# Reordering the edges of a four-layer linear-attention and gated-MLP kernel: first tiles, norms, o tiles, last product

## Chip, cores, metric

One core of a Trainium2 chip. The metric is the device time in microseconds (us) of one execution, lower is better. PE is the matmul engine, DVE the vector engine, ACT the activation engine, POOL the general one, SP the queue that issues the DMAs. SBUF is the on-chip memory, PSUM the one that takes PE's sums. The granted clock is the share of PE's full clock that the profile shows. Tiles, groups and units are counted from 0: k(2,0) is the first half of tile 2's k product.

## The reference, cut

Four layers over x of 2048 x 1024 in bf16: A, B, A, B, each on a layer norm of x and added to x.

```python
def _A_ref(x, wqkv, wo):                 # linear attention, 32 heads of 32
    q, k, v = ...x @ wqkv...
    pq, pk = phi(q), phi(k)              # t > 0: t + 1, else exp(t); + 1e-6
    kv = jnp.einsum("bhsd,bhse->bhde", pk, v)
    z = jnp.einsum("bhsd->bhd", pk)
    num = jnp.einsum("bhqd,bhde->bhqe", pq, kv)
    den = jnp.einsum("bhqd,bhd->bhq", pq, z)[..., None] + 1e-6
    return (num / den)... @ wo
def _B_ref(x, w_gate, w_up, w_down):     # F = 3584
    return ((x @ w_gate) * (x @ w_up)) @ w_down
x = x + _A_ref(_layernorm(x), A_wqkv, A_wo); x = x + _B_ref(_layernorm(x), ...)   # twice
```

## The kernel before

x stays in SBUF as 16 tiles of 128 rows (four groups of four). A matmul unit accumulates 8 (or 28) matmuls of 512 columns into one of four PSUM buffers ("mm"); a fifth PSUM tile ("kv", one buffer) takes the kv products and later the o tiles. The order of the program is set by hand: lists of units, woven together: `weave(main, fill, first, step)` puts one piece of `fill` after unit `first` of `main` and after every `step`-th one from there, and the rest of `fill` at the end. In the traces the instructions of an engine follow each other in the order in which the units are called, on DVE also where a later one is ready first: in that of before ACT's part of a phi is done at 837.79 us, and DVE's part of it starts at 845.03, behind the statistics and applies called ahead of it. So the call order is read here as the queue order of each engine.

```python
def ln_stats(t):    # DVE: bn_stats twice, bn_aggr; POOL: add eps, power -0.5
def ln_apply(t):    # DVE: xn = (X[t] - mean) * rstd
def tx_pe(t):       # PE: eight 128x128 transposes of xn into PSUM; ACT: copy to xT
def tx(t, slot):    # the same transpose as one DMA on SP
def phi(ps, dst):   # ACT: e = exp(ps); DVE: e = min(e, 1) + 1e-6; dst = max(ps + 1 + 1e-6, e)
def k_unit(t, n):   # 8 matmuls, phi
def v_unit(t, n):   # 8 matmuls, ACT copy
def kv_unit(t):     # 8 matmuls of 132 columns into kv; after the last tile DVE: KVz = kv * mask
def q_unit(g, c):   # 8 matmuls, phi into pqT[g % 3]
def o_unit(t):      # 8 matmuls of 132 columns with KVz into kv; DVE: den + 1e-6, reciprocal, divide
def d_unit(t, n, last): # 28 matmuls, DVE: X += ps, and in the last layer the store

# ---- start of layer 0 (cut) ----
for t in range(TPG):                  # TPG = 4
    ln_stats(t)
    if t > 0:
        ln_apply(t - 1)
ln_apply(3)
ones()
make_mask()
tx_pe(0)()
for t in range(TPG):
    k_unit(t, 0)()
    if t < 3:
        tx_pe(t + 1)()
ts = range(TPG)
main = [k_unit(t, 1) for t in ts] + [v_unit(t, 0) for t in ts]
# ... v_unit(t, 1) and kv_unit(t - 1) follow
fill = []
for t in range(TPG, 2 * TPG):
    fill += [stats_unit(t), apply_unit(t), tx_pe(t)]
do(weave(main, fill, 1, 1))

# ---- o phase (cut) ----
do([q2[0], kv_unit(NT - 1), q2[1], q2[2], o0[0], q2[3], q2[4], o0[1], t0[0], q2[5], o0[2], t0[1], q2[6],
    q2[7], o0[3], ...])

# ---- last group of the down-projection, layer 1 (cut) ----
main = d_unit(t, 0), d_unit(t, 1), stats_unit(t) for each of the four tiles
fill = norm_fill(1, 1, True) + norm_fill(2, 2, True)     # 24 pieces: statistics, applies, transposes
do(weave(main, fill, 0, 1))                              # one piece after each unit, the rest at the end
```

Of the kernel before, what the change touches and what calls it, by code (L numbers as in the profile page):

```python
# [9 lines left out]
ALU = mybir.AluOpType  # L10
# [15 lines left out]
def kernel(  # L26
# [11 lines left out]
    nc = tc.nc  # L38
# [56 lines left out]
    def load(dst, src):  # L95
        nc.sync.dma_start(out=dst, in_=src)  # L96
# [7 lines left out]
    def load_q():  # L104
        for n in range(2):
            load(wq[n], wqkv_v[:, :, n * NB:(n + 1) * NB])

    def load_o():
        for n in range(2):
            load(wo[n], wo_v[:, :, n * NB:(n + 1) * NB])  # L110
# [7 lines left out]
        for i in range(KF // 4):  # L118
            load(Dr[i][:].rearrange("p (f n) -> p f n", n=D), wd_v[:, 4 * i:4 * i + 4, :])

    load(X[:, 0, :], x_view[:, 0, :])
    load(X[:, 1, :], x_view[:, 1, :])
    for k in range(0, KD, 2):
        load(wk[0][:, k:k + 2, :], wqkv_v[:, k:k + 2, D:D + NB])
    load(X[:, 2, :], x_view[:, 2, :])
    load(X[:, 3, :], x_view[:, 3, :])
    load_k(1)
    load_v(0)
    load_v(1)
    for t in range(TPG, 2 * TPG):  # L130
        load(X[:, t, :], x_view[:, t, :])
    load_q()
    for t in range(2 * TPG, NT):
        load(X[:, t, :], x_view[:, t, :])
    load_o()


    ident = const.tile([P, P], BF16, tag="ident", name="ident")
# [22 lines left out]
    def ln_stats(t):  # L161
        st = small.tile([P, 2, 6], F32, tag="st", name="st")
        for c in range(2):
            nc.vector.bn_stats(out=st[:, c, :], in_=X[:, t, c * NB:(c + 1) * NB])  # L164
        mv = small.tile([P, 2], F32, tag="mv", bufs=2 * TPG, name="mv")
        nc.vector.bn_aggr(out=mv[:], in_=st[:])
        ve = small.tile([P, 1], F32, tag="ve", name="ve")
        nc.gpsimd.tensor_scalar(out=ve[:], in0=mv[:, 1:2], scalar1=1e-5, scalar2=None, op0=ALU.add)
        rstd = small.tile([P, 1], F32, tag="rstd", bufs=2 * TPG, name="rstd")
        nc.gpsimd.tensor_tensor(out=rstd[:], in0=ve[:], in1=mhalf[:], op=ALU.pow)  # L170
        stat[t] = (mv, rstd)
# [3 lines left out]
    def ln_apply(t):  # L175
        mv, rstd = stat.pop(t)
        xn = work.tile([P, D], BF16, tag="xn", name="xn")
        nc.vector.tensor_scalar(out=xn[:], in0=X[:, t, :], scalar1=mv[:, 0:1], scalar2=rstd[:],
                                op0=ALU.subtract, op1=ALU.mult)
        xns[t] = xn  # L180
# [13 lines left out]
    def tx_pe(t):  # L194

        def run():
            if t not in xns:
                ln_apply(t)
            src = xns.pop(t)
            pt = psum.tile([P, KD, P], BF16, tag="mm", bufs=MM, name="pt")  # L200
            for k in range(KD):
                nc.tensor.transpose(out=pt[:, k, :], in_=src[:, k * P:(k + 1) * P], identity=ident[:])  # L202
            nc.scalar.copy(out=xT[t // TPG][:, :, t % TPG * P:(t % TPG + 1) * P], in_=pt[:])  # L203
        return run

    def mm_tile():
        return psum.tile([P, NB], F32, tag="mm", bufs=MM, name="ps")
# [15 lines left out]
    def k_unit(t, n):  # L223
        def run():
            ps = mm_tile()
            xt, tl = xT[t // TPG], t % TPG
            for k in range(KD):
                nc.tensor.matmul(out=ps[:], lhsT=xt[:, k, tl * P:(tl + 1) * P], rhs=wk[n][:, k, :],  # L228
                                 start=(k == 0), stop=(k == KD - 1))
            phi(ps, pk[t % 4][:, n * NB:(n + 1) * NB])  # L230
        return run
# [61 lines left out]
    def add_x(t, n, ps):  # L293
        nc.vector.tensor_tensor(out=X[:, t, n * NB:(n + 1) * NB], in0=X[:, t, n * NB:(n + 1) * NB],  # L294
                                in1=ps[:], op=ALU.add)
# [25 lines left out]
        return run  # L321

    def d_unit(t, n, last):
        def run():
            ps = mm_tile()
            tl = t % TPG
            for f in range(KF):
                nc.tensor.matmul(out=ps[:], lhsT=hT[:, f, tl * P:(tl + 1) * P], rhs=wd[f][:, n * NB:(n + 1) * NB],  # L328
                                 start=(f == 0), stop=(f == KF - 1))
            add_x(t, n, ps)  # L330
            if last:
                nc.sync.dma_start(out=o_view[:, t, n * NB:(n + 1) * NB], in_=X[:, t, n * NB:(n + 1) * NB])
        return run

    def stats_unit(t):
# [22 lines left out]
    def ones():  # L358
        for i in range(4):
            nc.gpsimd.memset(vz[i][:, :, P:ZW], 1.0)  # L360
# [8 lines left out]

    def layer_A(li):  # L370
        if li == 0:
            for t in range(TPG):
                ln_stats(t)
                if t > 0:
                    ln_apply(t - 1)
            ln_apply(3)
            ones()
            make_mask()
            tx_pe(0)()
            for t in range(TPG):  # L380
                k_unit(t, 0)()
                if t < 3:
                    tx_pe(t + 1)()
            ts = range(TPG)
            main = [k_unit(t, 1) for t in ts] + [v_unit(t, 0) for t in ts]
            for t in ts:
                main.append(v_unit(t, 1))
                if t > 0:
                    main.append(kv_unit(t - 1))
            fill = []  # L390
            for t in range(TPG, 2 * TPG):
                fill += [stats_unit(t), apply_unit(t), tx_pe(t)]
            do(weave(main, fill, 1, 1))
        else:
            ones()
            do(weave(kv_group(0), norm_fill(3, 3, False), 1, 2))
        do(weave(kv_group(1), norm_fill(2, 2, True) if li == 0 else [], 1, 1))
        do(q_group(0))
        do(weave(kv_group(2), norm_fill(3, 3, True) if li == 0 else [], 1, 1))
        do(q_group(1))  # L400
        do(kv_group(3))
        load_gu(0)
        load_gu(1)

        def o(g):
            return [o_unit(t) for t in range(g * TPG, (g + 1) * TPG)]

        def to(g):
            return [to_unit(t) for t in range(g * TPG, (g + 1) * TPG)]

        def out_group(g):
            return [u for t in range(g * TPG, (g + 1) * TPG) for u in (out_unit(t, 0), out_unit(t, 1))]

        o0, t0, o1, t1, o2, t2, o3, t3 = o(0), to(0), o(1), to(1), o(2), to(2), o(3), to(3)
        q2, q3 = q_group(2), q_group(3)
        do([q2[0], kv_unit(NT - 1), q2[1], q2[2], o0[0], q2[3], q2[4], o0[1], t0[0], q2[5], o0[2], t0[1], q2[6],
            q2[7], o0[3], t0[2], q3[0], q3[1], q3[2], o1[0], t0[3], q3[3], q3[4], o1[1], t1[0], q3[5],
            q3[6], o1[2], t1[1], q3[7]])
        s = [stats_unit(t) for t in range(TPG)]
        a = [apply_unit(t) for t in range(TPG)]  # L420
        x = [tx(t, 0) for t in range(TPG)]
        u = out_group(0)
        do([u[0], o1[3], t1[2], u[1], u[2], o2[0], t1[3], u[3], u[4], o2[1], u[5], u[6], o2[2], u[7]])
        u = out_group(1)
        do([t2[0], t2[1], t2[2], u[0], o2[3], u[1], t2[3], s[0], u[2], o3[0], u[3], s[1], u[4], o3[1], u[5], s[2],
            u[6], o3[2], u[7], s[3]])
        load_gu(2)
        u = out_group(2)
        do([t3[0], t3[1], u[0], o3[3], t3[2], u[1], a[0], u[2], t3[3], x[0], u[3], a[1], u[4], x[1], u[5], a[2],
            u[6], x[2], u[7], a[3]])  # L430
        do([x[3]] + out_group(3))

    def layer_B(li):
        last = li == 3
        load_d()
        nxt = norm_fill(1, 1, True)
        for g in range(NG):
            main = []
            for fb in range(FB):
                i = g * FB + fb  # L440
                main += [gu_unit(i, fb * 4 + j) for j in range(4)]
                main.append(prefetch(i, last))
            do(weave(main, nxt, 2, 1))
            nxt = []
            main = []
            for tl in range(TPG):
                t = g * TPG + tl
                main += [d_unit(t, 0, last), d_unit(t, 1, last)]
                if g == NG - 1 and not last:
                    main.append(stats_unit(t))  # L450
            if g == 0:
                nxt = norm_fill(2, 0, True)
            elif g == 1:
                nxt = norm_fill(3, 1, True)
            elif g == 2 and not last:
                nxt = norm_fill(0, 0, True)
            fill = []
            if g == 3 and not last:
                fill = norm_fill(1, 1, True) + norm_fill(2, 2, True)
            do(weave(main, fill, 0, 1))  # L460
        if not last:
            load_q()
            load_o()
# [48 lines left out]
```

## Time and profile before

1659.57 us median of four runs (1659.42 to 1659.61). The page of the profiled execution, its first two lines and the chain of waits by engine (busy us, share of the span, instructions):

```profile
span 1657.6 us, 18876 instructions
PE 1643.1 (99%) x8016; PEld 761.1 (46%) x8016; DVE 537.5 (32%) x963; ACT 254.1 (15%) x426; POOL 53.7 (3%) x152
PE 97%; DVE 1%; ACT 0%; DMA 0%; SPq 0%; issue 0%; POOL 0%; POOLq 0%
```

PE is the limit and hardly ever rests. Matmuls overlap (one of 512 columns is recorded as 379 ns long), so the 1643 us alone do not prove it, but the starts do: 216 ns from one 512-column matmul to the next and 56 ns for 128 columns. All that an order of instructions can win is the time in which PE stands. PE's own waits before (who waited for whom: us in total, times, longest):

```profile
PE ps L228 <- ACT xT_70 L203: 4.5, 4, 1.1
PE kv L276 <- DVE H L281: 2.6, 2, 1.3
PE pt L202 <- DVE xn L178: 2.0, 3, 1.3
PE zps L156 <- DVE xT_73 L153: 1.2, 1, 1.2
PE kv L252 <- DVE H L220: 0.8, 2, 0.5
```

This is the whole prize, about 10 us (the 1.2 us of zps, the dummy matmuls before X 0 lands, are no part of it; from start to start of the matmuls each gap is some 0.15 us longer than the wait as the page counts it, at the o tile 1.45 against 1.29). L228 is a k unit waiting for the copied transpose, L202 a transpose waiting for xn, L276 an o tile, L252 a kv product. PE's timeline of the start (start us, us, then the instructions; in brackets the idle time before):

```profile
6.76 0.62 PE L202 MATMUL pt<-ident,xn 128*128 128x128 bf16 x8 [0.28 <-DVE xn L178]
8.48 1.90 PE L228 MATMUL ps<-W_74,xT_70 128*128 128x512 bf16 x8 [1.10 <-ACT xT_70 L203]
10.80 0.62 PE L202 MATMUL pt<-ident,xn 128*128 128x128 bf16 x8 [0.42 <-DVE xn L178]
12.52 1.90 PE L228 MATMUL ps<-W_74,xT_70 128*128 128x512 bf16 x8 [1.10 <-ACT xT_70 L203]
29.66 0.62 PE L202 MATMUL pt<-ident,xn 128*128 128x128 bf16 x8 [1.35 <-DVE xn L178]
```

Each k unit has only its own tile, so PE waits four times for transpose and copy; at 29.66 tile 4's transpose waits for xn, whose statistics stood behind phi on DVE. The o phase of the first A layer (timeline):

```profile
168.45 0.63 PE L276 MATMUL kv<-KVz,D_80 128*128 128x132 bf16 x8
172.37 0.63 PE L276 MATMUL kv<-KVz,D_80 128*128 128x132 bf16 x8
174.74 1.23 DVE L281 TENSOR_TENSOR H<-kv,den 128x1024 bf16<-128x1024 f32 x1
176.02 0.64 PE L276 MATMUL kv<-KVz,D_80 128*128 128x132 bf16 x8 [1.29 <-DVE H L281]
```

Two q units lie between the first two o tiles and one between the second and third; the third needs the kv buffer, which DVE frees at 175.97. The second A layer begins like this:

```profile
846.10 0.41 PE L252 MATMUL kv<-H 128*128 128x132 bf16 x4 [0.31 <-DVE H L220]
847.03 0.41 PE L252 MATMUL kv<-H 128*128 128x132 bf16 x4 [0.52 <-DVE H L220]
```

The first kv product waits twice for phi (L220), which stood on DVE behind statistics and applies (836.07 to 845.12 us). And the tail:

```profile
1654.27 0.69 DVE L294 TENSOR_TENSOR X<-X,ps 128x512 bf16<-128x512 bf16 x1 [5.36 <-PE ps L328]
1654.99 0.33 SPq L332 DMA_DIRECT2D out_dram<-X  x1
```

The last add takes 0.69 us, and its store lands 1.70 us after its issue, at 1656.69.

### The profile page before, as it was taken

The numbers are of one execution on the slowest core, as the hardware profiler recorded it, in microseconds if no ns is written. First come the engines' busy times: TensorE is split into PE (matmuls) and PEld (weight loads), VectorE is DVE, ScalarE is ACT, GpSimd is POOL, SyncE is SP. The second block draws the span as 40 slices with busy tenths as digits, with TensorE's granted clock in tenths as the row PEclk, the third lists the DMA queues.
The fourth block names the chain that finished last, engine by engine and source line by source line (L and its number), as shares of the span: only waits on it lengthen the run. The fifth ranks groups of instructions, "written<-read, shape, count | busy, mean of one in ns | idle before, by whom it ended". The sixth has DMA issues, their size and how long they took to land.

```text
span 1657.6 us, 18876 instructions
## 1 busy us (share of the span) xinstructions
PE 1643.1 (99%) x8016; PEld 761.1 (46%) x8016; DVE 537.5 (32%) x963; ACT 254.1 (15%) x426; POOL 53.7 (3%) x152
## 2 busy tenths in 40 slices
PE   8999999999999999999999999999999999999999
PEld 3544444444444444444444445444444444444444
DVE  5453873211311321131353348631122113111111
ACT  3333201100110110011023331011001101100110
POOL 2000000000000000000110000000000000000000
PEclk9999999999999999999999999999999999999999
DMA  9111459530641353063260033594225405421400
GB/s 304 27 26 55 105 121 288 168 102 4 178 152 48 111 169 102 3 179 102 66 159 1 0 109 66 134 307 152 86 69 173 156 23 156 154 85 64 153 4 23
DMA packets 240483, 181.57 MB, mean 110 GB/s; under 512 B 96016, under 2 KB 231184, under 8 KB 240400
## 3 DMA queue, kind: packets, MB, share of 16 engines
q1 hardware_dynamic: 240400, 180.38, 37.6%
q8 instruction: 62, 1.02, 0.3%
q14 instruction: 21, 0.17, 0.0%
HBM read 153.09 MB, written 4.19 MB: 95 GB/s over the span
## 4 chain that ended last, share of the span: by engine, by line
PE 97%; DVE 1%; ACT 0%; DMA 0%; SPq 0%; issue 0%; POOL 0%; POOLq 0%
PE ps L316 47%; PE ps L328 23%; PE ps L302 7%; PE ps L265 6%; PE ps L238 6%; PE ps L228 6%; PE kv L252 1%; PE kv L276 1%; DVE st L164 1%; DMA X<-in_A_x_dram 0%; ACT xT_70 L203 0%; ACT H L218 0%; SPq L96 0%; PE pt L202 0%; DVE H L281 0%
## 5 line engine op out<-in xcount | busy, mean ns | idle before, releaser
L320 DVE TENSOR_TENSOR H<-gs,ps 128x512 bf16<-128x512 f32 x224 | 154.0, 688 | 567.7 <-PE ps L316 563.1
L319 ACT COPY gs<-ps 128x512 f32<-128x512 f32 x224 | 131.0, 585 | 1048.1 <-PE ps L316 1048.1
L328 PEld LDWEIGHTS <-H 128*128 128x128 bf16 x1792 | 175.3, 98 | 211.5
L294 DVE TENSOR_TENSOR X<-X,ps 128x512 bf16<-128x512 bf16 x128 | 87.3, 683 | 359.1 <-PE ps L328 330.4
L218 ACT ACTIVATE H<-ps 128x512 bf16<-128x512 f32 x128 | 76.4, 597 | 208.3 <-PE ps L228 99.6
L316 PEld LDWEIGHTS <-W_75 128*128 128x128 bf16 x640 | 62.6, 98 | 75.5
L316 PEld LDWEIGHTS <-W_74 128*128 128x128 bf16 x640 | 62.6, 98 | 75.5
L219 DVE TENSOR_SCALAR H<-H 128x512 bf16<-128x512 bf16 x128 | 37.3, 291 | 168.4 <-ACT H L218 168.4
L316 PEld LDWEIGHTS <-xT_73 128*128 128x128 bf16 x576 | 56.4, 98 | 67.9
L316 PEld LDWEIGHTS <-xT_72 128*128 128x128 bf16 x576 | 56.4, 98 | 68.0
L316 PEld LDWEIGHTS <-W_77 128*128 128x128 bf16 x576 | 56.4, 98 | 67.9
L316 PEld LDWEIGHTS <-W_76 128*128 128x128 bf16 x576 | 56.3, 98 | 68.0
L164 DVE BATCH_NORM_STATS2 st<-X 128x6 f32<-128x512 bf16 x128 | 80.9, 674 | 4.3 <-DMA X<-in_A_x_dram 4.3
L316 PE MATMUL ps<-xT_71,W_77 128*128 128x512 bf16 x320 | 75.6, 379 | 0.0
L316 PE MATMUL ps<-xT_71,W_74 128*128 128x512 bf16 x320 | 75.6, 379 | 0.0
L316 PE MATMUL ps<-xT_70,xT_72 128*128 128x512 bf16 x320 | 75.6, 379 | 0.0
L316 PE MATMUL ps<-xT_70,xT_73 128*128 128x512 bf16 x320 | 75.6, 379 | 0.0
L316 PE MATMUL ps<-xT_70,W_75 128*128 128x512 bf16 x320 | 75.6, 379 | 0.0
L316 PE MATMUL ps<-xT_71,W_76 128*128 128x512 bf16 x320 | 75.6, 379 | 0.0
L316 PE MATMUL ps<-xT_71,W_75 128*128 128x512 bf16 x320 | 75.6, 379 | 0.0
L316 PE MATMUL ps<-xT_70,W_74 128*128 128x512 bf16 x320 | 75.6, 379 | 0.0
L302 PEld LDWEIGHTS <-H 128*128 128x128 bf16 x512 | 49.4, 98 | 56.2
(88 smaller groups left out, 1715.0 us busy)
## 6 DMA issues: line engine op xcount, KB each, us to landing
W_74<-in_B_w_gate_dram SPq DMA_DIRECT2D x20, 1024.0 KB, 5.3
W_75<-in_B_w_up_dram SPq DMA_DIRECT2D x20, 1024.0 KB, 7.2
W_76<-in_B_w_gate_dram SPq DMA_DIRECT2D x18, 1024.0 KB, 5.3
W_77<-in_B_w_up_dram SPq DMA_DIRECT2D x18, 1024.0 KB, 7.3
xT_72<-in_B_w_gate_dram SPq DMA_DIRECT2D x18, 1024.0 KB, 5.3
xT_73<-in_B_w_up_dram SPq DMA_DIRECT2D x18, 1024.0 KB, 7.4
X<-in_A_x_dram SPq DMA_DIRECT2D x16, 256.0 KB, 7.8
out_dram<-X SPq DMA_DIRECT2D x32, 128.0 KB, 1.7
```

The costliest lines, as they stand in the source:

```text
L164: nc.vector.bn_stats(out=st[:, c, :], in_=X[:, t, c * NB:(c + 1) * NB])
L218: nc.scalar.activation(out=e, in_=ps[:], func=ACT.Exp)
L219: nc.vector.tensor_scalar(out=e, in0=e, scalar1=1.0, scalar2=1e-6, op0=ALU.min, op1=ALU.add)
L228: nc.tensor.matmul(out=ps[:], lhsT=xt[:, k, tl * P:(tl + 1) * P], rhs=wk[n][:, k, :], start=(k == 0), stop=(k == KD - 1))
L238: nc.tensor.matmul(out=ps[:], lhsT=xt[:, k, tl * P:(tl + 1) * P], rhs=wv[n][:, k, :], start=(k == 0), stop=(k == KD - 1))
L265: nc.tensor.matmul(out=ps[:], lhsT=wq[n][:, k, cl * P:(cl + 1) * P], rhs=xT[g][:, k, :], start=(k == 0), stop=(k == KD - 1))
L294: nc.vector.tensor_tensor(out=X[:, t, n * NB:(n + 1) * NB], in0=X[:, t, n * NB:(n + 1) * NB], in1=ps[:], op=ALU.add)
L302: nc.tensor.matmul(out=ps[:], lhsT=oT[(t // TPG) % 2][:, c, tl * P:(tl + 1) * P], rhs=wo[n][:, c, :], start=(c == 0), stop=(c == KD - 1))
L316: nc.tensor.matmul(out=ps[:], lhsT=w[:, k, j * P:(j + 1) * P], rhs=xT[g % 2][:, k, :], start=(k == 0), stop=(k == KD - 1))
L319: nc.scalar.copy(out=gs[:], in_=gp[:])
L320: nc.vector.tensor_tensor(out=hT[:, f, :], in0=gs[:], in1=up[:], op=ALU.mult)
L328: nc.tensor.matmul(out=ps[:], lhsT=hT[:, f, tl * P:(tl + 1) * P], rhs=wd[f][:, n * NB:(n + 1) * NB], start=(f == 0), stop=(f == KF - 1))
```

## The change

The intent is to take PE's waits away at four places: (1) the start: other order of the first loads and tiles, group 1's transposes by DMA instead of PE, the loads of wq, X 8 to 15 and wo after them; (2) the norms of the next A layer spread over the last down-projection, four pieces after each unit, instead of one piece a unit and the rest after it, with the statistics of group 3 moved from there into the A layer; (3) an o tile at every second q unit; (4) the last product in three parts, so that the last add and store are small.

```diff
-    load(X[:, 0, :], x_view[:, 0, :])
-    load(X[:, 1, :], x_view[:, 1, :])
+    load_x(0)
     for k in range(0, KD, 2):
         load(wk[0][:, k:k + 2, :], wqkv_v[:, k:k + 2, D:D + NB])
+        if k == 0:
+            load_x(1)
...                        (load_q, X 8 to 15 and load_o move behind the start, below)
     def d_unit(t, n, last):
+        parts = [(0, 256), (256, 384), (384, 512)] if last and (t, n) == (NT - 1, 1) else [(0, NB)]
...                        (matmuls, add and store once for each part)
         if li == 0:
-            (as printed above)
+            ln_stats(0)
+            ln_stats(1)
+            ln_apply(0)
+            ln_apply(1)
+            tx_pe(0)()
+            tx_pe(1)()
+            ln_stats(2)
+            ln_apply(2)
+            k_unit(0, 0)()
+            ln_stats(3)
+            ln_apply(3)
+            k_unit(1, 0)()
+            tx_pe(2)()
+            k_unit(0, 1)()
+            tx_pe(3)()
             ones()
             make_mask()
+            main = [k_unit(2, 0), k_unit(1, 1), k_unit(3, 0), k_unit(2, 1), k_unit(3, 1)]
+            main += [v_unit(t, 0) for t in ts]
...
+            do(weave(main, norm_fill(1, 1, True), 3, 1))     # DMA transposes
+            load_q()
+            for t in range(2 * TPG, NT):
+                load_x(t)
+            load_o()
         else:
             ones()
-            do(weave(kv_group(0), norm_fill(3, 3, False), 1, 2))
+            do(weave(kv_group(0), norm_fill(3, 3, True), 1, 2))
...
-        do([q2[0], kv_unit(NT - 1), q2[1], q2[2], o0[0], q2[3], q2[4], o0[1], t0[0], q2[5], o0[2], t0[1], q2[6], ...
+        do([q2[0], kv_unit(NT - 1), q2[1], o0[0], q2[2], q2[3], o0[1], t0[0], q2[4], q2[5], o0[2], t0[1], q2[6], ...
...                        (statistics of the last group leave the down-projection of layer B)
-            do(weave(main, fill, 0, 1))
+            for i, u in enumerate(main):
+                u()
+                do(fill[4 * i:4 * i + 4])
```

More of the change, by code (lines that the diff above doesn't have):

```diff
@@ L119, in load_d, with load_x @@
             load(Dr[i][:].rearrange("p (f n) -> p f n", n=D), wd_v[:, 4 * i:4 * i + 4, :])
-    load(X[:, 0, :], x_view[:, 0, :])
-    load(X[:, 1, :], x_view[:, 1, :])
+    def load_x(t):
+        load(X[:, t, :], x_view[:, t, :])
+    load_x(0)
     for k in range(0, KD, 2):
         load(wk[0][:, k:k + 2, :], wqkv_v[:, k:k + 2, D:D + NB])
-    load(X[:, 2, :], x_view[:, 2, :])
-    load(X[:, 3, :], x_view[:, 3, :])
+        if k == 0:
+            load_x(1)
+    load_x(2)
+    load_x(3)
     load_k(1)
@@ L130 @@
     for t in range(TPG, 2 * TPG):
-        load(X[:, t, :], x_view[:, t, :])
-    load_q()
-    for t in range(2 * TPG, NT):
-        load(X[:, t, :], x_view[:, t, :])
-    load_o()
+        load_x(t)
     ident = const.tile([P, P], BF16, tag="ident", name="ident")
@@ L323, in d_unit @@
     def d_unit(t, n, last):
+        parts = [(0, 256), (256, 384), (384, 512)] if last and (t, n) == (NT - 1, 1) else [(0, NB)]
         def run():
-            ps = mm_tile()
             tl = t % TPG
-            for f in range(KF):
-                nc.tensor.matmul(out=ps[:], lhsT=hT[:, f, tl * P:(tl + 1) * P], rhs=wd[f][:, n * NB:(n + 1) * NB],
-                                 start=(f == 0), stop=(f == KF - 1))
-            add_x(t, n, ps)
-            if last:
-                nc.sync.dma_start(out=o_view[:, t, n * NB:(n + 1) * NB], in_=X[:, t, n * NB:(n + 1) * NB])
+            for lo, hi in parts:
+                ps = mm_tile()
+                cols = slice(n * NB + lo, n * NB + hi)
+                for f in range(KF):
+                    nc.tensor.matmul(out=ps[:, 0:hi - lo], lhsT=hT[:, f, tl * P:(tl + 1) * P], rhs=wd[f][:, cols],
+                                     start=(f == 0), stop=(f == KF - 1))
+                nc.vector.tensor_tensor(out=X[:, t, cols], in0=X[:, t, cols], in1=ps[:, 0:hi - lo], op=ALU.add)
+                if last:
+                    nc.sync.dma_start(out=o_view[:, t, cols], in_=X[:, t, cols])
         return run
@@ L371, in layer_A @@
         if li == 0:
-            for t in range(TPG):
-                ln_stats(t)
-                if t > 0:
-                    ln_apply(t - 1)
+            ln_stats(0)
[8 more added lines that the diff above has]
+            ln_stats(3)
             ln_apply(3)
+            k_unit(1, 0)()
+            tx_pe(2)()
+            k_unit(0, 1)()
+            tx_pe(3)()
             ones()
             make_mask()
-            tx_pe(0)()
-            for t in range(TPG):
-                k_unit(t, 0)()
-                if t < 3:
-                    tx_pe(t + 1)()
             ts = range(TPG)
-            main = [k_unit(t, 1) for t in ts] + [v_unit(t, 0) for t in ts]
+            main = [k_unit(2, 0), k_unit(1, 1), k_unit(3, 0), k_unit(2, 1), k_unit(3, 1)]
+            main += [v_unit(t, 0) for t in ts]
             for t in ts:
@@ L389, in layer_A @@
                     main.append(kv_unit(t - 1))
-            fill = []
-            for t in range(TPG, 2 * TPG):
-                fill += [stats_unit(t), apply_unit(t), tx_pe(t)]
-            do(weave(main, fill, 1, 1))
+            do(weave(main, norm_fill(1, 1, True), 3, 1))
+            load_q()
+            for t in range(2 * TPG, NT):
+                load_x(t)
+            load_o()
         else:
             ones()
-            do(weave(kv_group(0), norm_fill(3, 3, False), 1, 2))
+            do(weave(kv_group(0), norm_fill(3, 3, True), 1, 2))
         do(weave(kv_group(1), norm_fill(2, 2, True) if li == 0 else [], 1, 1))
@@ L415, in layer_A @@
         q2, q3 = q_group(2), q_group(3)
-        do([q2[0], kv_unit(NT - 1), q2[1], q2[2], o0[0], q2[3], q2[4], o0[1], t0[0], q2[5], o0[2], t0[1], q2[6],
-            q2[7], o0[3], t0[2], q3[0], q3[1], q3[2], o1[0], t0[3], q3[3], q3[4], o1[1], t1[0], q3[5],
-            q3[6], o1[2], t1[1], q3[7]])
+        do([q2[0], kv_unit(NT - 1), q2[1], o0[0], q2[2], q2[3], o0[1], t0[0], q2[4], q2[5], o0[2], t0[1], q2[6],
+            q2[7], o0[3], t0[2], q3[0], q3[1], o1[0], t0[3], q3[2], q3[3], o1[1], t1[0], q3[4], q3[5], o1[2], t1[1],
+            q3[6], q3[7]])
         s = [stats_unit(t) for t in range(TPG)]
@@ L444, in layer_B @@
             nxt = []
-            main = []
-            for tl in range(TPG):
-                t = g * TPG + tl
-                main += [d_unit(t, 0, last), d_unit(t, 1, last)]
-                if g == NG - 1 and not last:
-                    main.append(stats_unit(t))
+            main = [d_unit(g * TPG + tl, n, last) for tl in range(TPG) for n in range(2)]
+            fill = []
             if g == 0:
@@ L456, in layer_B @@
                 nxt = norm_fill(0, 0, True)
-            fill = []
-            if g == 3 and not last:
+            elif g == 3 and not last:
                 fill = norm_fill(1, 1, True) + norm_fill(2, 2, True)
-            do(weave(main, fill, 0, 1))
+            for i, u in enumerate(main):
+                u()
+                do(fill[4 * i:4 * i + 4])
         if not last:
```

## The prediction

> **What bounds it.** PE. The page gives it 1643 of 1657.6 us; the chain of waits is 97% PE. Start to start, a 512-column matmul takes 216 ns and a 128-column one 56 ns at granted clock 1.0 [...]. From the first transpose (6.76 us) to the last matmul nearly all is matmuls at that pitch. The timeline and PE's waits show only about 10 us in which PE stands, and the change can win little more.
>
> Where PE stands before:
> - Start, 6.8 to 46.7 us: 5.8 us in four tile-by-tile waits (xn on DVE, copy on ACT), and 1.5 us at 27.9 us for tile 4's transpose, whose statistics queued behind phi on DVE.
> - Second o tile, 174.4 and 993.2 us: 1.45 us each. One q unit lies between o tiles 1 and 2, and the single kv PSUM tile is held until DVE has divided.
> - Start of the second A layer, 845 us: 1.2 us; the first kv product waits for phi, which queued behind four statistics.
> - Tail: add 0.69 us, store 1.70 us from issue to landing.
>
> **The change, costed.**
> 1. Start. X tile 1 now lands third (about 5.5 us instead of 4.0). Statistics of both tiles precede the first apply in DVE's queue, so the first transpose slips from 6.76 to about 7.4. Then two k units run together. X tile 2 lands as before (8.8): statistics, POOL power, apply take 2.7 us, then phi 1.0, statistics of tile 3 2.6, apply 0.5: tile 3's transpose waits 1.2 us (to 16.1) and k(2,0) another 0.5 us for the buffer that k(1,0)'s phi frees (17.05). From there 13 units of 1.73 us and three kv products of 0.48 us without waits: kv group 1 starts at about 41.0 instead of 46.65. Of these 5.65 us, 1.8 are the four PE transposes (0.45 each) that become DMA transposes. Loads of wq and X 8-15 now come behind those; X8 lands near 47.5, some 1.3 us after DVE wants it, but the buffer it holds up is needed at about 55.7 and free at 54: no loss.
> 2. Norms spread: all 24 fills are done by the sixth down-projection unit (6.05 us each, DVE at most 6.4 us in one), and DVE is clear at the boundary: -1.15.
> 3. o tiles at every second q unit: the 1.45 us wait goes, since a cycle of 3.93 us covers DVE's 3.6. But o tile 0 comes one q unit earlier (166.7) and the masked KVz is ready only at 167.55 on DVE: a new wait of about 0.87. Net -0.6 a layer, -1.2 in all. The intent is mostly given back here.
> 4. Last product in 256+128+128 columns: +0.14 us of PE (an estimate: 28 x (109+56+56) ns against 28 x 216), last add about 0.28 instead of 0.69, a store of rows of 256 B little quicker: -0.35.
>
> Sum -8.35. Predicted 1651.2 us; 8 in 10 between 1649.3 and 1653.2. Faster by over 2%: 0.5%; within 2%: 99%; slower: 0.5%.
>
> **To check.** First transpose near 7.4; waits at tile 3's transpose and k(2,0), 13 to 17 us; kv group 1 near 41; no PE wait at 845 less 6; an o wait of 0.8 to 0.9 us in each A layer, now at the first o tile, ended by KVz; after the last matmul about 3 us instead of 3.4.
>
> **What would make it wrong.** X8 landing over 1.5 us later than I think (PE waits in kv group 1); a cold clock after the longer idle at 6.5 to 9 us; o tiles after the first with less margin than 0.3 us; a slow 256 B store.

The 216 and 56 ns are those of the trace. The sum: -5.65 - 1.15 - 1.2 - 0.35 = -8.35. The 109 ns for 256 columns in term 4 was an estimate and lies on the straight line through 56 ns for 128 columns and 216 for 512; the trace of after shows 109. The cold clock is named as a risk only: in the trace of before the dummy matmuls at the start follow each other every 0.43 us up to 4.57 us and every 0.22 us after it; that the slow pace can come back after a stretch in which PE stands much is shown later, by e12 alone.

## The result

1650.41 us median of four runs (1649.99 to 1650.60), in the stated range and 0.8 us under the stated figure. A ratio is the mean time of one kernel's runs over that of the other's of the same rounds, so not quite the ratio of the medians quoted: 0.9945, interval 0.9927 to 0.9962. That is the same by the 2% measure, and clear of no change. The page after, the same lines:

```profile
span 1648.8 us, 18785 instructions
PE 1632.5 (99%) x7882; PEld 762.9 (46%) x8040; DVE 537.9 (33%) x965; ACT 250.6 (15%) x422; POOL 53.8 (3%) x152
PE 98%; DVE 1%; issue 1%; DMA 0%; SPq 0%; POOL 0%; ACT 0%
```

Some 2% of the matmul records are missing in this trace (7882 of 8040), so the busy time of PE is not compared. PE's waits after:

```profile
PE pt L202 <- DVE xn L178: 2.7, 3, 1.5
PE kv L276 <- DVE KVz L256: 1.4, 2, 0.7
PE zps L156 <- DVE xT_73 L153: 1.2, 1, 1.2
```

Two of the five lines are gone; the o wait has stayed as a line but has another releaser. The timeline of the start:

```profile
7.48 0.62 PE L202 MATMUL pt<-ident,xn 128*128 128x128 bf16 x8 [0.52 <-DVE xn L178]
8.79 0.62 PE L202 MATMUL pt<-ident,xn 128*128 128x128 bf16 x8 [0.70 <-DVE xn L178]
9.25 3.62 PE L228 MATMUL ps<-W_74,xT_70 128*128 128x512 bf16 x16
12.71 0.61 PE L202 MATMUL pt<-ident,xn 128*128 128x128 bf16 x8
16.50 0.62 PE L202 MATMUL pt<-ident,xn 128*128 128x128 bf16 x8 [1.46 <-DVE xn L178]
16.95 1.89 PE L228 MATMUL ps<-W_74,xT_70 128*128 128x512 bf16 x8
48.52 1.29 DVE L164 BATCH_NORM_STATS2 st<-X 128x6 f32<-128x512 bf16 x2 [1.93 <-DMA X<-in_A_x_dram]
```

The first transpose is later (7.48 against 6.76), then two k units run together; the largest wait left is the transpose of tile 3. The last line is DVE waiting 1.93 us for X tile 8: no wait of PE answers to it. The o phase:

```profile
160.43 1.25 DVE L256 TENSOR_TENSOR KVz<-kv,mask 128x1056 bf16<-128x1056 f32 x1
161.73 0.63 PE L276 MATMUL kv<-KVz,D_80 128*128 128x132 bf16 x8 [0.71 <-DVE KVz L256]
165.65 0.63 PE L276 MATMUL kv<-KVz,D_80 128*128 128x132 bf16 x8
169.56 0.63 PE L276 MATMUL kv<-KVz,D_80 128*128 128x132 bf16 x8
```

Now the first o tile waits, for KVz, and the next ones follow every 3.92 us without a wait. From start to start of the matmuls the new gap is 0.87 us, the old one 1.45. The second A layer and the tail:

```profile
838.59 0.69 DVE L220 SCALAR_TENSOR_TENSOR H<-ps,H 128x512 bf16<-128x512 f32 x1
839.16 0.63 PE L252 MATMUL kv<-H 128*128 128x132 bf16 x8
1646.17 0.29 DVE L335 TENSOR_TENSOR X<-X,ps 128x128 bf16<-128x128 bf16 x1 [1.28 <-PE ps L333]
1646.49 0.33 SPq L337 DMA_DIRECT2D out_dram<-X  x1
```

The first kv product runs in one piece. The last add takes 0.29 us, and its store lands at 1647.92, 1.43 us after its issue.

Where the 8.81 us between the two spans come from can be read by equal work: the time at which the same piece of work starts in both traces.

| start of | before | after | difference | step |
|---|---|---|---|---|
| third kv product (end of the first group) | 46.21 | 40.34 | -5.87 | start -5.87 |
| last kv product, first A layer | 164.53 | 158.66 | -5.87 | nothing lost in between |
| second layer (weights of its first product) | 254.89 | 248.43 | -6.46 | o tiles -0.59 |
| third layer | 835.05 | 828.59 | -6.46 | |
| last kv product, third layer | 983.33 | 975.69 | -7.64 | norms -1.18 |
| fourth layer | 1073.70 | 1065.46 | -8.24 | o tiles -0.60 |
| last down-projection unit | 1647.81 | 1639.58 | -8.23 | |
| end | 1657.64 | 1648.83 | -8.81 | last product -0.58 |

### The profile page after: what moved, and what is told of

It reads as the page before. It is cut to its first block, busy times and chain, and to the rows that moved or that the text cites. A ratio compares the mean times of both kernels' runs of the same rounds, so it can differ in the third digit from the quotient of the medians.

```text
span 1648.8 us, 18785 instructions
## 1 busy us (share of the span) xinstructions
PE 1632.5 (99%) x7882; PEld 762.9 (46%) x8040; DVE 537.9 (33%) x965; ACT 250.6 (15%) x422; POOL 53.8 (3%) x152
## 4 chain that ended last, share of the span: by engine, by line
PE 98%; DVE 1%; issue 1%; DMA 0%; SPq 0%; POOL 0%; ACT 0%
PE ps L316 47%; PE ps L333 23%; PE ps L238 7%; PE ps L302 7%; PE ps L265 6%; PE ps L228 6%; PE kv L276 1%; PE kv L252 1%; DMA X<-in_A_x_dram 0%; SPq L96 0%; DVE st L164 0%; DVE KVz L256 0%; DVE D_82 L220 0%; ACT H L218 0%; DVE xn L178 0%
## 5 line engine op out<-in xcount | busy, mean ns | idle before, releaser
L335 DVE TENSOR_TENSOR X<-X,ps 128x512 bf16<-128x512 bf16 (+1 forms) x66 | 44.2, 670 | 327.0 <-PE ps L333 296.5
```

Of the source, the lines that this page charges most:

```text
L335: nc.vector.tensor_tensor(out=X[:, t, cols], in0=X[:, t, cols], in1=ps[:, 0:hi - lo], op=ALU.add)
```

## The experiments

Theory: the four steps add up, each by the wait it removes; of the start's gain 1.8 us is PE work and the rest waits; the o step is mostly given back because KVz stands behind phi on DVE. Rivals are named with each run. Twelve runs were made, all with correct results; "before" is the median of the kernel before on the same chip.

| run | us median (range) | before | ratio |
|---|---|---|---|
| e1_start_only | 1653.41 (1653.28 to 1654.14) | 1659.64 | 0.9963 |
| e2_norms_only | 1658.37 (1658.05 to 1658.76) | 1659.64 | 0.9992 |
| e3_o_order_only | 1658.60 (1658.30 to 1658.73) | 1659.64 | 0.9993 |
| e4_parts_only | 1659.28 (1659.00 to 1659.56) | 1659.64 | 0.9997 |
| e5_pe_transposes | 1652.55 (1651.98 to 1653.21) | 1659.53 | 0.9958 |
| e6_loads_early | 1650.47 (1650.02 to 1651.10) | 1659.53 | 0.9946 |
| e7_kvz_first | 1649.90 (1648.52 to 1651.54) | 1659.53 | 0.9942 |
| e8_stats3_first | 1649.97 (1649.52 to 1650.58) | 1659.53 | 0.9942 |
| e9_after_again | 1650.85 (1650.08 to 1651.26) | 1659.87 | 0.9945 |
| e10_x1_second | 1650.16 (1649.91 to 1650.40) | 1659.87 | 0.9942 |
| e11_all_three | 1647.11 (1646.77 to 1647.49) | 1659.87 | 0.9923 |
| e12_before_x1_third | 1660.51 (1660.01 to 1662.06) | 1659.87 | 1.0007 |

Every interval is about 0.0025 wide, so by time alone the runs with a difference of about 1 us are not clear of each other or of no change (e2, e3, e4, e12 against before); for those the traces decide, by equal work as above.

### Each step alone: e1 to e4

Each is the kernel before with one of the four hunks of the diff (start; norms; o order; parts), nothing else.

> Only the new load order and the new order of the first tiles (with the DMA transposes for group 1 and the later loads); the rest as before. If the parts do not act on each other, the start gives what the two traces show between the first transpose and the second q group: 5.9 us less than before, about 1653.7 us. If the start only looks so good because of what follows it (rival: the parts lean on each other), the gain is below 5 or above 6.5 us.

> Only the norms of the next A layer spread over the last down-projection. Expected: 1.15 to 1.2 us less than before (about 1658.4), the two PE waits for phi in the second A layer's first kv product (0.48 and 0.68 us) gone, no new wait. Rival: DVE gets too full inside the down-projection and PE waits there for a PSUM buffer: then the gain is smaller and PE waits at the product's line between 790 and 835 us.

> Only the o tiles at every second q unit. Expected: net 0.6 us a layer, 1.2 us in all (about 1658.4): the 1.45 us wait at the third o tile goes, a wait of 0.87 us at the first one, ended by KVz on DVE, comes. Rival (what the change was meant for): the whole 2.9 us.

> Only the last product in 256+128+128 columns. Expected from the two traces: 0.58 us less than before (about 1659.0): 0.13 us more on PE, 0.40 less in the last add, 0.27 less from the issue of the last store to its landing, 0.16 less from the last matmul's start to the add. My prediction on record had 0.35.

Measured: 6.23, 1.27, 1.04 and 0.36 us under before, 8.90 in sum, against 9.16 for the whole change (1659.57 less 1650.41). So the steps add up, and the rival of e1 falls. In e2 PE has no wait between 780 and 860 us, so DVE is not too full. In e3 the new wait is there without the new start, in both A layers (the line "PE kv L276 <- DVE KVz L256: 1.4, 2, 0.7" is in its waits too): the new wait belongs to the o order itself. e4 fell short of its expectation: in its trace the stretch from the last unit to the end is 9.50 us, against 9.83 before and 9.25 after, so this step gives 0.33 to 0.58 us. The difference between e4 and after is the store (1.50 and 1.43 us to landing) and the end of the program after it (1.08 and 0.91). The small store landed 1.43 to 1.50 us after its issue in the nine profiles that have it, the large one 1.70 to 1.71 in the other five. The two differ in size (32 and 128 KB) and in the length of their rows (256 B and 1 KB), so the effect of the rows alone is not shown. The terms of the expectation add up to 0.70 and not to 0.58: its 0.16 for the last matmul is already in the 0.13 of PE (see below, last product).

### What the start's gain is made of: e5

```diff
-            do(weave(main, norm_fill(1, 1, True), 3, 1))
+            fill = norm_fill(1, 1, True)
+            for i, t in zip((6, 8, 10, 11), range(TPG, 2 * TPG)):
+                fill[i] = tx_pe(t)
+            do(weave(main, fill, 3, 1))
```

> The kernel after with the four transposes of tile group 1 on PE again (as before), all else left. Expected: 1.8 us slower than after (four times 0.45 us of PE, no new wait), about 1652.2 us: this share of the start's gain is PE work taken away, the other 4.1 us are waits. Rival: the transposes on PE also cost waits, as one of them did before (1.5 us); then over 3 us slower.

Measured: 1652.55 us, 2.1 above the first median of after, at an interval that does not part this from 1.8. The trace does: the third kv product starts 32.78 us after X 2 has landed (41.51 less 8.73), against 31.00 in after, which is 1.78 more (why X 2 is the mark to count from stands under e8). PE has no wait between 18 and 46 us in it. So the transposes moved to DMA are worth their PE time (four times 0.45 us) and no more; the other 4.1 us of the start are waits.

### The place of the loads: e6

```diff
     for t in range(TPG, 2 * TPG):
         load_x(t)
+    load_q()
+    for t in range(2 * TPG, NT):
+        load_x(t)
+    load_o()
...                        (and the same taken out behind the start)
```

> The kernel after with the loads of wq, X 8 to 15 and wo back in their old place, ahead of the DMA transposes in the queue. My theory: that X 8 now lands 2 us after DVE wants it costs nothing, since PE has buffers; so nothing is won, and the transposes for group 1 land later, behind the bulk loads: 0 to 0.7 us slower than after. Rival: the late X 8 costs time; then this is about 1 us or more faster than after.

Measured: 1650.47 us, ratio 0.9946, as after. DVE's wait for X 8 is gone (X 8 has landed at 28.84 us), and the span does not move; the first DMA transpose, behind the bulk loads in the queue, lands at 40.44 us, just before PE wants it at 40.80. So the moved loads neither cost nor win here. There is little room, though: in e10, where the start is faster, DVE's wait for X 8 grows to 2.6 us and a matmul unit of PE at 54.5 us waits 0.33 us from start to start (0.2 as the page counts it).

### The new o wait: e7

```diff
-    def q_unit(g, c):
+    def q_unit(g, c, between=None):
...                        (after the 8 matmuls)
+            if between is not None:
+                between()
             phi(ps, pqT[g % 3][:, c, :])
...
-        do([q2[0], kv_unit(NT - 1), q2[1], o0[0], ...
+        do([q_unit(2, 0, kv_unit(NT - 1)), q2[1], o0[0], ...
```

> The kernel after with the last kv product and the masking of KVz put ahead of phi of the first q unit of group 2, so that KVz comes first in DVE's queue; the same instructions. If the new 0.87 us wait at the first o tile is KVz standing behind phi on DVE, it goes to nearly nothing in both A layers: 1.6 to 1.75 us faster than after, about 1648.7. Rival: it is the end of the kv product itself or the kv PSUM tile, then no difference. Second risk: phi, now later, delays the division of the first o tile and the second o tile waits instead.

Measured: 1649.90 us, which alone would have said that about a third of the gain came (0.5 us of 1.6 to 1.75). The timeline says otherwise:

```profile
160.28 1.26 DVE L256 TENSOR_TENSOR KVz<-kv,mask 128x1056 bf16<-128x1056 f32 x1 [4.40 <-PE kv L252]
161.81 0.63 PE L278 MATMUL kv<-KVz,D 128*128 128x132 bf16 x8
```

DVE now stands ready before the kv product ends, KVz is done in time, and the o tile follows with no wait; none appears at the later o tiles either. By equal work the stretch from group 2's first q product to the first out-projection is 31.36 us against 32.23, 0.87 less, in both A layers. The cause of the new wait is thereby shown: KVz behind phi in DVE's queue. (In the trace of after the kv product ends at 159.29 us and KVz starts only at 160.43, after both instructions of phi.) What ate the gain is at the start of the same run: kv product three starts at 41.25 us, 0.91 later than in the profile of after.

### The largest wait left, and what hid it: e8

```diff
             ln_stats(2)
+            ln_stats(3)
             ln_apply(2)
             k_unit(0, 0)()
-            ln_stats(3)
             ln_apply(3)
```

> The kernel after with the statistics of tile 3 ahead of the apply of tile 2 on DVE, where DVE idles for POOL's power anyway. If the 1.4 us wait at tile 3's transpose comes from its statistics standing behind apply and phi on DVE, it goes, against 0.2 us more before tile 2's transpose: 1.2 to 1.4 us faster than after, about 1649.1. Rival: it is the landing of X 3 or the load of the second k weights that holds the start; then no gain, and PE waits for a DMA at the third k unit.

Measured: 1649.97 us, less than expected; the expectation failed as a time. Tile 3's transpose has no wait any more, and PE waits for no DMA at its third k unit, so the rival falls. But the first transpose waits longer (1.66 us; 0.52 in after):

```profile
6.95 1.29 DVE L164 BATCH_NORM_STATS2 st<-X 128x6 f32<-128x512 bf16 x2 [1.88 <-DMA X<-in_A_x_dram]
8.95 0.62 PE L202 MATMUL pt<-ident,xn 128*128 128x128 bf16 x8 [1.66 <-DVE xn L178]
```

X tile 1 landed at 6.93 us in this profile (5.45 in that of after). In the new order it is the third load of the program. In the eight profiles of kernels with it third it landed at 5.34, 5.37, 5.45, 6.00, 6.08, 6.40, 6.91 and 6.93 us; in the six with it second, at 3.96 to 4.31. (X 2, the seventh load in both orders, moves too: 8.32 to 9.68 us over all fourteen.) DVE takes the statistics of tile 1 ahead of the apply of tile 0, so all of PE's start hangs on it. The start of the third kv product can be written as the later of two chains, worked out from these profiles: X 1's landing plus 34.35 us, or X 2's landing plus 31.00 us.

| profile | X 1 | X 2 | later chain | measured |
|---|---|---|---|---|
| after | 5.45 | 9.34 | 40.34 (X 2) | 40.34 |
| e1 | 6.40 | 9.24 | 40.75 (X 1) | 40.73 |
| e6 | 6.00 | 8.86 | 40.35 (X 1) | 40.34 |
| e7 | 6.91 | 9.63 | 41.26 (X 1) | 41.25 |
| e9 | 5.34 | 8.83 | 39.83 (X 2) | 39.82 |
| e10 | 4.18 | 8.51 | 39.51 (X 2) | 39.50 |

The constants were fitted on after, e1, e5, e6 and e7 for the load of group 1's first weights, 0.40 us later (expectation of e9, 34.75 and 31.4); e9 and e10 came later and fit. Against e7, whose X 1 was as late, e8 starts the third kv product at 40.17 instead of 41.25: the reordered statistics do win 1.1 us.

### Settling it: e9 to e12

e9 is the kernel after unchanged. e10 loads X 1 second again. e11 is e10, e8 and e7 together. e12 is the kernel before with X 1 third. The edit of e10 (e12 is its reverse):

```diff
     load_x(0)
+    load_x(1)
     for k in range(0, KD, 2):
         load(wk[0][:, k:k + 2, :], wqkv_v[:, k:k + 2, D:D + NB])
-        if k == 0:
-            load_x(1)
```

> The kernel after once more, to see how far it moves by itself and for comparison on this chip. The profiles so far show the third load of the program landing anywhere from 5.4 to 6.9 us, and in the new order that is X tile 1, which the first apply waits for. Expected: about 1650.4 us, runs over a range of about 1 us or more; in the profile kv group 1 starts at the later of X 1's landing plus 34.75 us and X 2's landing plus 31.4 us (worked out from the profiles of after, e1, e5, e6, e7).

> The kernel after with only the old order of the first loads (X 1 ahead of the first part of the weights). Expected: X 1 lands near 4.0 and the first transpose is at 6.8 us, as in all kernels with that order; the start is then bound by X 2 alone (landing plus 31.4 us), so 0 to 0.9 us faster than after, about 1650.0, with less spread. Rival (what the new order was meant for): the first weights come later and hold the first k unit; then it is slower than after by half a us or more.

> X 1 second, statistics of tile 3 ahead of the apply of tile 2, and KVz ahead of phi, all on the kernel after. In e8 the gain of the second was hidden by X 1's late landing (6.9 us). Expected: kv group 1 starts at 38.6 to 39.2 us instead of 40.75 (the transpose of tile 3 and the one of tile 2 wait 0.2 us at most), and 0.87 us less in each o phase: 1646.7 to 1647.4 us in all. Rival: a new wait in place of the ones taken away, so that it stays above 1648.

> The kernel before with only the new order of the first loads. Expected from the same reading: it gains nothing; the first transpose slips from 6.8 to between 7.4 and 8.9 us and the total gets 0.2 to 1.2 us longer than before. Rival: earlier weights help; then it is faster than before.

Measured on one chip: after 1650.85, e10 1650.16 with less than half the range of runs. By the medians X 1 second is 0.7 us faster, at intervals that overlap. So no gain of the new order of loads shows, and it makes the start depend on one more landing that moves; the rival (early weights) falls, since the first k unit did not wait for weights in e10. e10 won less than its start alone would (the 0.33 us of X 8 above).

e12 is no faster than before, and two of its five runs, the profiled one among them, are the slowest (1661.91 and 1662.06 us, granted clock 0.999; the others 1660.01 to 1660.51 at 1.0). The trace of the first shows a stretch at half the clock (the second has no trace): busy time of each engine in three stretches, with the granted clock of PE after them:

```profile
6.43:9.85 3.42, 1.58 (x14) 0.67 (x12) 2.61 (x6) 1.01 (x1) 0.97 (x2) 1.00 1.04 353
9.85:13.26 3.42, 3.42 (x9) 1.21 (x10) 2.69 (x7) 0.00 (x0) 1.86 (x4) 0.50 1.10 359
13.26:16.70 3.44, 2.29 (x17) 1.22 (x16) 1.63 (x3) 1.50 (x2) 1.36 (x14) 1.00 1.10 348
```

(The first numbers are the length, then PE, weight loads, DVE, ACT and POOL with their counts, then the clock.) And PE's timeline there:

```profile
8.11 0.62 PE L203 MATMUL pt<-ident,xn 128*128 128x128 bf16 x8 [0.73 <-DVE xn L179]
9.83 3.58 PE L229 MATMUL ps<-W,xT 128*128 128x512 bf16 x8 [1.10 <-ACT xT L204]
13.22 0.64 PE L203 MATMUL pt<-ident,xn 128*128 128x128 bf16 x8
```

With X 1 landing at 6.08 us PE was busy for 1.58 of 3.42 us, with no wait over 1.1 us (in before for 2.04 us in the same stretch and for 2.50 of 3.41 from 4.60 to 8.01 us); the clock then went to half for 3.41 us, and the k unit took 3.39 us from its start to the next instruction instead of 1.73, as two lines above show. Stretches of 3.41 us with PE busy for 1.74 us (e1, 5.14 to 8.55 us) and 2.04 (e6, 7.34 to 10.75 us) are in profiled runs whose mean clock is 1.0. That the stretch with little PE work brought the half clock is read from their order in this one trace, which gives no threshold. Of the kernels with X 1 third, two had such runs: e12 (two of five) and e7, whose slowest run, 1651.54 us, is its only one with the clock 0.999 (it has no trace, so its cause is argued, not shown). No run of a kernel with X 1 second had one, nor did after in its nine runs.

e11: 1647.11 us, all five runs under all five of after on the same chip, in the expected range. PE's waits:

```profile
PE zps L155 <- DVE xT L152: 1.2, 1, 1.2
PE pt L201 <- DVE xn L177: 1.0, 2, 0.7
```

and its start:

```profile
12.67 1.89 PE L227 MATMUL ps<-W,xT 128*128 128x512 bf16 x7
14.40 0.61 PE L201 MATMUL pt<-ident,xn 128*128 128x128 bf16 x8
```

The o waits and that of tile 3's transpose are gone. It is the best version found: 3.7 us faster than after, 12.8 faster than before. Left open: whether the early loads of e6 added to e11 would save the tenths that X 8 can cost; that was not run. That X 2's landing binds the start is read from the fit and from DVE's waits; the loads of X 2 and X 3 ahead of the weights were not tried.

## Why the prediction was right

The time, 1650.41, lies in 1649.3 to 1653.2, and each step but one wait, that at k(2,0), was where the text put it. Point by point:

- **What bounds it: right.** PE stays at its pitch (216 and 56 ns in the trace of after too), and only waits and four transposes were won.
- **Start, -5.65 predicted, -5.87 measured; e1 confirms it alone.** The first transpose at 7.48 (about 7.4 predicted) and the 1.8 us of transposes (e5) are as predicted, and the wait at tile 3's transpose came (1.46 us, 1.2 predicted). But two errors cancelled, so part of the closeness is luck. X 2 landed at 9.34 and not "as before (8.8)", which made tile 3's transpose 16.50 instead of 16.1. And the wait of 0.5 us at k(2,0) for "the buffer that k(1,0)'s phi frees" did not come: the unit started at 16.95, right after the transpose, while phi of k(1,0) ran on DVE to 17.38. In the built program that unit has the PSUM buffer of tile 2's transpose, not that of k(1,0), and its first matmul has no wait for DVE in the trace; I had assumed that the four buffers go round strictly.
- **X 1 at "about 5.5": right for the profile of after, wrong as a constant.** It lies anywhere from 5.3 to 6.9, and I counted only one fixed landing. This is the part of the change that works against its purpose (e10, e12).
- **X 8: landing 47.5 predicted, 48.49 measured, DVE waits 1.93 us, PE does not.** Right in its effect, with e6 as its test, and with less room than I claimed.
- **Norms, -1.15 predicted, -1.18 measured; e2 alone -1.27 by time.** Right. What stood ahead of phi was more than the "four statistics" of the text: five and four applies.
- **o tiles, -0.6 a layer predicted, -0.59 and -0.60 measured.** Right with its cause: the wait of 0.87 us for KVz is what I predicted, and e7 takes it away. One word is loose: before, it is the third o tile that waits, not the second.
- **Last product, -0.35 predicted, -0.58 in after, -0.33 in e4.** The mechanism was right; the term mis-sized is the store. The PE estimate, +0.14, was right (the three parts' stretch of 28 matmuls each is 6.18 us against 6.05), and so was the last add (0.29 instead of 0.69). This leaves 0.08 of the predicted 0.35 us for the store ("little quicker"), which landed 0.27 us sooner in after (1.43 instead of 1.70) and 0.20 in e4. From the start of the last matmul to the add it is 0.42 us before and 0.25 after, but this is no further gain: the shorter last matmul (56 ns instead of 216) is already in the 6.18.
- **A cold clock**, named as a risk, did not hit after (clock 1.0 in its nine runs), but hit e12 (0.50 for 3.41 us in the profiled run), and by its clock figure of 0.999 one run of e7; both have the load order of after. A slow store of 256 B rows did not come: the last one landed in 1.43 us.

The sum of the steps, -8.35, was 0.46 us short of the spans' -8.81: 0.22 at the start, 0.23 at the tail.

## What to carry to other kernels

Where one engine is busy all the time, count its gaps first: they are the whole prize, and each gap is worth what its own timeline says. When a unit is moved earlier to fill one gap, work out what it will wait for at its new place, and look at the order in the queue of the engine that releases it: putting the releasing instruction one place ahead (KVz before phi: 0.87 us in each A layer; statistics before an apply that waits anyway: 1.1 us) won as much here as the move of the o tiles (0.59 and 0.60 us). What the first instructions of a program wait for should be the first loads issued: X 1 landed at 3.96 to 4.31 us as the second load (six profiles) and at 5.34 to 6.93 as the third (eight). A single profile does not show such a range: compare several.
